# A gated linear recurrence and an ELU layer on one Trainium2 core: the decay chain of the next unit moved to other places in the order of work

## The chip, the cores and the metric

The program runs on one core of one Trainium2 chip. Its engines work side by side, each on its own queue, in order: TensorE (PE; its weight loads are listed apart as PEld), VectorE (DVE), ScalarE (ACT), GpSimd (POOL) and SyncE (SP), which here only issues DMAs. An engine that waits holds everything behind it in its queue. The metric is the device time of one execution in microseconds (us), the median of several runs.

## The reference

The first half is a linear recurrence with complex decays, for 4 batches, 8 heads, 768 steps and 48 channels a head. The second is a two-layer network with ELU between the layers, over the 3072 tokens that come out.

```python
mag = np.sqrt(a_re * a_re + a_im * a_im)
scale = np.minimum(mag, 0.999) / (mag + 1e-06)
a_re_n, a_im_n = (a_re * scale, a_im * scale)
for t in range(S):
    ar, ai = (a_re_n[:, :, t, :, None], a_im_n[:, :, t, :, None])
    new_re = ar * S_re - ai * S_im
    new_im = ar * S_im + ai * S_re
    kv = np.einsum('bhd,bhe->bhde', k[:, :, t], v[:, :, t])
    S_re, S_im = (new_re + kv, new_im)
    y[:, :, t] = np.einsum('bhd,bhde->bhe', q[:, :, t], S_re)
...
x = np.ascontiguousarray(attn_out.transpose(0, 2, 1, 3)).reshape(B * S, H * D)
h = x @ w_in            # 3072x384 by 384x2048
g = np.where(h > 0.0, h, alpha * (np.exp(np.minimum(h, 0.0)) - 1.0))
return (g @ w_out).astype(np.float32)   # 2048x384
```

## The kernel before

**Units and layers.** The work is cut into 12 units, numbered u = 0 to 11. A unit is 128 steps of two batches, all 8 heads: 256 tokens. Each unit goes through two stages. Its *front* computes the recurrence for those 128 steps. Its *layer* runs the ELU network over its 256 tokens. The front of unit u is worked during the layers of u-2 and u-1, so that TensorE always has matrix products to do.

**The front, in its steps** (function names as in the code):

- `load_a`, `load_v`, `load_qk` fetch the inputs, four or two DMAs each on SP's queue. The decays' real and imaginary parts (`ar`, `ai`) have one buffer each.
- `squares` (L709, L710): two ScalarE squares. `joined` (L716): their sum, on GpSimd for units from 3 on.
- `logarithms` (L735, L736): two ScalarE logarithms, of `ar` and of the sum. `powers` (L746, L747): two ScalarE exponentials of these.
- `lengths` (L772, VectorE): the log of the capped decay, `l`. `ratios` (L759, L760, GpSimd), `slopes` (L780, VectorE), `angles` (L815, ScalarE arctangent), `carried` (L821, VectorE) and `noted` (L796, L799, VectorE minima and maxima).
- `turns`: a TensorE sum over time of the angles (L832), rounded by VectorE (L837, L840), and the last row sent on by a GpSimd-issued DMA (`carry`, L856). `waves` (L967 to L971): sine and cosine on ScalarE.
- `scaled` (L981 GpSimd, L982 VectorE), `ends` (L951, two DMAs issued by GpSimd) and `gated` (L993, keys on GpSimd, queries on VectorE) build the gated queries and keys.
- `transposed` (L1013 TensorE, L1014 ScalarE), `scored` (L1054, L1125), then `valued`: value products (L1087), the sums of the logs of the *next* unit (`quartered`, L883, which read `l`), the carried products (L1096), the exponentials of those sums (L898, ScalarE, in `quarters_used`) and the copies of the result to SBUF (L1156, L1157, ScalarE). `seam` (L1169) then moves a part of that result across partitions with six DMAs on SP's queue. Only then is the layer's input `x` complete.

**The layer.** `hidden` is eight steps: `inner` (12 matmuls, L1189, into one of three PSUM buffers tagged `mlp`) and `elu` (L1198 and L1199 on ScalarE, L1200 on VectorE). The second product is done by a scheme with seven products k = 1 to 7 in the place of eight, each in two halves h = 0, 1 (`product`, L1295, eight matmuls a half). The order is (1,0), (4,0), (1,1), (4,1), (6,0), (6,1), (5,0), (5,1), (7,0), (7,1), (2,0), (2,1), (3,0), (3,1), as pairs (k,h). `folded` (L1273, VectorE) prepares sums of the first matrix. The products use three `mlp` banks. Products 1, 2 and 6 share the first one. After (1,1) ScalarE copies product 1 out of it into a tile `ee` (L1303):

```python
if k == 1:
    x["u"] = new("ee", 2, [C, 2, GT])
    nc.scalar.copy(out=x["u"][:, 0, 0:HN], in_=to)
    return
```

Four quarters of the result go out through two `o` buffers, by DMAs on SP's queue (L1317). The third quarter is copied to its buffer by ScalarE (L1314) after (2,1), the others come from VectorE (L1316). The first `inner` of the next layer takes over the `mlp` bank that L1314 reads.

**What sets the order.** There is no scheduler at run time. Every step is given a place, a number of slots, by `put`; the list is sorted by place (ties in the order in which they were put) and the instructions are issued in that order, each to its engine's queue. A unit has 16 slots: with r = 16 (u-2), the layer of u-2 has its eight `hidden` at r+4 to r+11 and its fourteen half products from r+12 to r+19.4, and the layer of u-1 the same 16 slots later. Up to the first products of layer 2 a list written by hand (`first`) takes the place of the numbers; it holds all of the units 0 to 3, and of unit 4 the loads, squares, sum, logarithms and powers. `PAIRED` is 4. So the chain of unit 5 is the first that the numbers place from its squares on; this chain lies in layer 3, and that of unit 11, the last, in layer 9.

Of the kernel before, what the change touches and what calls it, by code (L numbers as in the profile page):

```python
# [505 lines left out]
def kernel(  # L506
# [19 lines left out]
    NU = B // NB * (S // C)  # L526
# [472 lines left out]
    PAIRED = 4  # L999
# [404 lines left out]
    def put(at, fn, *args):  # L1404
        if fn is hidden:
            plan.append((at, len(plan), inner, args))
            plan.append((at, len(plan), elu, args))
        else:
            plan.append((at, len(plan), fn, args))

    def decays_of(u, *at):
        fns = squares, logarithms, powers, lengths, ratios, slopes, noted, angles, carried
        put(at[0], begun, u)
        for x, fn in zip(at, fns):
            put(x, fn, u)
            if fn is squares:
                put(x, joined, u)

    def gates_of(u, *at):
        for x, fn in zip(at, (decays, turns, waves, scaled, ends, gated)):  # L1420
            if fn is not decays or u <= PAIRED:
                put(x, fn, u)

    def values_of(u, *at):
        fns = (transposed, "q"), (transposed, "k"), (scores,), (states,), (values,)
        for n in range(NB):
            for x, (fn, *key) in zip(at[5 * n :], fns):
                put(x, fn, u, *key, n)
        put(at[-1], seam, u)
# [64 lines left out]
    def layer_of(u, at_h, at_p):  # L1494
        for m in range(NF // 2):
            put(at_h[m], hidden, u, 2 * m)
        put(at_h[3], folded, u, 0)
        put(at_h[7], folded, u, 1)
        ks = [(1, 0), (4, 0), (1, 1), (4, 1)] + [(k, h) for k in (6, 5, 7, 2, 3) for h in range(2)]
        for m, (k, h) in enumerate(ks):  # L1500
            put(at_p[0] + m * len(at_p) / len(ks), product, u, k, h)

    for u in range(2, NU):
        r = (u - 2) * SLOTS
        put(r + 8, load_a, u)
        put(r + 8, load_v, u)
        put(r + 8, load_qk, u)
        if u == 2:
            decays_of(u, 16, 17, 17, 18.4, 19.5, 19.6, 22.7, 19.8, 19.8)
            gates_of(u, 20.4, 21.6, 22.1, 22.4, 22.4, 22.6)  # L1510
        else:
            decays_of(u, r + 11, r + 12, r + 12, r + 13.4, r + 13.5, r + 14.9, r + 16.7, r + 15.5, r + 16.6)
            gates_of(u, r + 15, r + 18, r + 18.5, r + 18, r + 18, r + 19.5)
        if u < PAIRED:
            values_of(u, *(max(r + 22, 24.5) + x for x in (0, 1, 2, 3, 5, 4, 5, 6, 7, 8, 9)))
        else:
            for n in range(NB):
                put(r + 22 + 2 * n, transposed, u, "q", n)
                put(r + 23 + 2.3 * n, transposed, u, "k", n)
            put(r + 26.6, scored, u)  # L1520
            put(r + (31 if u + 1 < NU else 29.3), valued, u)
            put(r + (31 if u + 1 < NU else 29.3), seam, u)
        layer_of(u, range(r + 36, r + 44), range(r + 44, r + 52))
    for m in range(NR):
        put(40 + 4 * m, test_fetch, m)
# [42 lines left out]
```

## Time and profile before

| what | value |
|---|---|
| median of 3 runs | 730.74 us (727.02 to 731.93) |
| the profiled execution: its own time | 733.4 us |
| its span, first to last instruction | 731.7 us |
| mean granted TensorE clock | 0.966 |
| TensorE busy | 677.1 us, 93% |
| weight loads busy | 593.2 us, 81% |
| ScalarE, VectorE, GpSimd busy | 398.5, 395.9, 176.0 us |

The profile is of one execution. Busy shares are averages over stages with different limits, and what an engine loses is read from the waits: for each group of instructions, how long its engine sat idle before it, and which instruction of which engine ended that. In rows of the order in time, the columns are start, length, engine, line, operation, tiles written and read, shapes, and how many were merged into the row; a bracket at the end is the idle time before it. PEclk is the clock that was granted to TensorE as a share of full speed.

### The profile page before, as it was taken

What the parts mean: (1) busy time and instruction counts of PE and PEld (TensorE: products, weight loads), DVE (VectorE), ACT (ScalarE), POOL (GpSimd) and SP (SyncE); (2) the same over time, 40 slices, a digit from 0 to 9 for tenths busy, and PEclk for the clock granted to TensorE, in tenths of its full rate; (3) what the DMA queues carried; (4) which work ended last, traced back from release to release, by engine and by line L of the source; (5) the groups of instructions that cost most, each with busy time, mean ns of one, the idle gap of its engine ahead of it and who ended that gap; (6) DMA issues with size and microseconds to landing.
All of it is one profiled execution on the core that took longest, in us unless ns stands there. A gap on an engine that the chain in (4) does not pass through costs nothing.

```text
span 731.7 us, 15769 instructions
## 1 busy us (share of the span) xinstructions
PE 677.1 (93%) x6656; PEld 593.2 (81%) x6656; DVE 395.9 (54%) x579; ACT 398.5 (54%) x622; POOL 176.0 (24%) x159
## 2 busy tenths in 40 slices
PE   8798899988999979979979998997997997999996
PEld 6787775665889879879879887997987986989995
DVE  5789999516666545454454553553644545433141
ACT  6765446578466456645653754655546654661230
POOL 2000000237145133151331431422413403310000
PEclk9889999999999989989999999998999999999999
DMA  9986555232536403701901901920730550200000
GB/s 166 168 144 110 141 172 130 51 61 50 77 77 110 93 23 88 115 22 49 154 23 40 142 23 33 152 41 25 125 77 22 116 86 24 72 1 7 22 1 27
DMA packets 149899, 55.98 MB, mean 77 GB/s; under 512 B 129172, under 2 KB 142652, under 8 KB 149820
## 3 DMA queue, kind: packets, MB, share of 16 engines
q1 hardware_dynamic: 147776, 54.32, 39.1%
q0 software_dynamic: 1824, 0.44, 0.8%
q8 instruction: 54, 0.88, 0.5%
q14 instruction: 25, 0.20, 0.1%
q10 hardware_dynamic: 220, 0.14, 0.1%
HBM read 48.88 MB, written 4.78 MB: 73 GB/s over the span
## 4 chain that ended last, share of the span: by engine, by line
PE 73%; issue 6%; ACT 5%; DVE 5%; POOL 5%; SPq 3%; DMA 2%; ACTq 0%; POOLq 0%; DVEq 0%
PE mlp L1189 28%; PE mlp L1295 22%; PE w L1013 5%; PE mlp L1210 4%; PE y L1096 3%; PE w L1054 2%; POOL n L716 2%; SPq L596 2%; PE y L1125 2%; PE y L1087 2%; PE w L832 2%; POOL S L1071 1%; PE w L1210 1%; ACT n L746 1%; ACT n L736 1%
## 5 line engine op out<-in xcount | busy, mean ns | idle before, releaser
L1189 PE MATMUL mlp<-x,w_in 128*128 128x256 f32 x1152 | 260.6, 381 | 2.6 <-DVE g L1200 2.6
L1189 PEld LDWEIGHTS mlp<-x,w_in 128*128 128x128 f32 x1152 | 214.6, 190 | 31.9 <-DVE g L1200 3.0
L1198 ACT ACTIVATE ee<-mlp 128x512 f32<-128x512 f32 x96 | 57.3, 597 | 144.1 <-PE mlp L1189 135.8
L1200 DVE SCALAR_TENSOR_TENSOR g<-ee,mlp 128x512 f32<-128x512 f32 x96 | 65.5, 685 | 126.2 <-ACT ee L1199 116.6
L1295 PE MATMUL mlp<-w_out,g 128*128 128x192 f32 x640 | 110.3, 326 | 0.0
L1295 PEld LDWEIGHTS mlp<-w_out,g 128*128 128x128 f32 x640 | 105.4, 190 | 2.7
L1295 PE MATMUL mlp<-w,g 128*128 128x192 f32 x320 | 70.5, 384 | 28.4 <-ACT ee L1303 28.4
L1295 PEld LDWEIGHTS mlp<-w,g 128*128 128x128 f32 x320 | 64.3, 227 | 31.9 <-ACT ee L1303 30.5
L1071 POOL TENSOR_TENSOR S<-S,T 128x384 f32<-128x384 f32 x36 | 29.3, 830 | 168.4 <-DVE S L1069 168.4
L1273 DVE TENSOR_TENSOR g<-g 128x512 f32<-128x512 f32 x80 | 67.2, 841 | 2.7
L1199 ACT ACTIVATE ee<-ee 128x512 f32<-128x512 f32 x96 | 60.5, 631 | 2.9
L898 ACT ACTIVATE n<-w 64x384 f32<-64x384 f32 (+1 forms) x60 | 28.1, 486 | 49.3 <-PE w L883 48.6
L856 POOL DMA_DIRECT2D carry<-n x10 | 5.3, 530 | 172.9 <-DVE n L840 172.9
L993 POOL TENSOR_TENSOR kg<-k,cs 128x1536 f32<-128x1536 f32 x9 | 41.0, 4551 | 20.1 <-issue 20.0
L1314 ACT COPY o<-mlp 128x192 f32<-128x192 f32 x10 | 3.2, 319 | 67.1 <-DMA out_dram<-o 56.3
L821 DVE SCALAR_TENSOR_TENSOR n<-carry,n 1x768 f32<-1x768 f32 x10 | 9.5, 946 | 45.3 <-ACT n L815 45.3
L1210 PE MATMUL mlp<-w_out,g 128*128 128x384 f32 x96 | 32.8, 490 | 0.7 <-DVE g L1200 0.7
L1014 ACT COPY qt<-w 128x512 f32<-128x512 f32 x48 | 25.6, 581 | 12.5 <-PE w L1013 12.5
L1295 PE MATMUL mlp<-wt,g 128*128 128x192 f32 x160 | 29.2, 327 | 0.0
L993 DVE TENSOR_TENSOR qg<-q,cs 128x1536 f32<-128x1536 f32 (+1 forms) x12 | 19.5, 1623 | 17.4 <-ACT cs L971 17.4
L716 POOL TENSOR_TENSOR n<-n 128x768 f32<-128x768 f32 x9 | 19.8, 2196 | 35.4 <-ACT n L710 35.4
L1013 PE MATMUL w<-ident,kg 128*128 128x128 f32 x192 | 26.0, 280 | 2.3 <-POOL kg L993 1.4
(173 smaller groups left out, 981.4 us busy)
## 6 DMA issues: line engine op xcount, KB each, us to landing
w<-in_moe_w_out_dram SPq DMA_DIRECT2D x8, 768.0 KB, 4.9
g<-in_moe_w_in_dram SPq DMA_DIRECT2D x16, 384.0 KB, 3.2
g<-in_moe_w_out_dram SPq DMA_DIRECT2D x16, 384.0 KB, 3.4
w<-in_moe_w_in_dram SPq DMA_DIRECT2D x16, 288.0 KB, 5.9
vn<-in_v_dram SPq DMA_DIRECT2D x24, 192.0 KB, 4.0
out_dram<-o SPq DMA_DIRECT2D x48, 96.0 KB, 2.1
ar<-in_a_re_dram SPq DMA_DIRECT2D x22, 192.0 KB, 4.6
ai<-in_a_im_dram SPq DMA_DIRECT2D x22, 192.0 KB, 7.5
```

The source lines that it names most:

```text
L716: products(u).tensor_tensor(out=x["m2"], in0=x["m2"], in1=x["sq"], op=ALU.add)
L898: nc.scalar.activation(out=flat(x[key][to, n : n + 1]), in_=t[of], func=AF.Exp, scale=sign)
L993: eng.tensor_tensor(out=to[:, :, :, 0:D], in0=each.unsqueeze(2).to_broadcast([C, step * H, 2, D]), in1=x["cs"][:, n * H : (n + step) * H], ...
L1013: nc.tensor.transpose(t[:, h], of, ident)
L1071: eng.tensor_tensor(out=new_s, in0=new_s, in1=wide, op=ALU.mult)
L1189: nc.tensor.matmul(t[:, e], lhsT=w_in[:, i, ts(f + e, C)], rhs=x["x"][:, i], start=(i == 0), stop=(i == NI - 1),)
L1198: nc.scalar.activation(out=e, in_=t, func=AF.Relu, scale=-1.0)
L1199: nc.scalar.activation(out=e, in_=e, func=AF.Exp, scale=-1.0)
L1200: nc.vector.scalar_tensor_tensor(out=x["g", f // 8][:, f % 8 : f % 8 + 2], in0=e, scalar=-1.0, in1=t, op0=ALU.add, op1=ALU.max)
L1210: nc.tensor.matmul(x["o", n], lhsT=x["g", f // 8][:, f % 8, ts(n, C)], rhs=w_out[:, f], start=(f == 0), stop=(f == NF - 1),)
L1273: nc.vector.tensor_tensor(out=S_of(u, k, h), in0=a, in1=b, op=op)
L1295: nc.tensor.matmul(to, lhsT=a[:, m], rhs=b[:, m], start=(first and h == 0 and m == 0), stop=False, skip_group_check=True,)
```

## The change

Five steps get other places. For units from 5 on:

- `load_a` is issued at the start of layer u-2 (r+4) and not in its middle (r+8).
- `squares` moves from the end of layer u-2's `hidden` (r+11, ahead of the first product) to r+7.2, behind its fourth `hidden`. `joined`, which shared the place of the squares, gets its own, r+8.4, behind the fifth.
- `powers` moves from r+12, right behind `logarithms`, to r+13.2: behind half product (1,1), and so behind that product's ScalarE copy (L1303), and ahead of (4,1).

For units from 4 on `valued` and `seam` move from r+31 to r+31.6, that is, from ahead of half product (5,0) to behind it, and with that from ahead of the next unit's `angles` to behind them (not for the last unit). `turns` moves from r+18 to r+18.6: behind half product (2,1), and behind `scaled` and `ends`, which it was ahead of. `waves` moves from r+18.5 to r+19, behind (3,0).

```diff
     def decays_of(u, *at):
-        fns = squares, logarithms, powers, lengths, ratios, slopes, noted, angles, carried
+        fns = squares, joined, logarithms, powers, lengths, ratios, slopes, noted, angles, carried
         put(at[0], begun, u)
         for x, fn in zip(at, fns):
             put(x, fn, u)
-            if fn is squares:
-                put(x, joined, u)
...
-        put(r + 8, load_a, u)
+        put(r + (4 if u > PAIRED else 8), load_a, u)
         put(r + 8, load_v, u)
         put(r + 8, load_qk, u)
         if u == 2:
-            decays_of(u, 16, 17, 17, 18.4, 19.5, 19.6, 22.7, 19.8, 19.8)
+            decays_of(u, 16, 16, 17, 17, 18.4, 19.5, 19.6, 22.7, 19.8, 19.8)
             gates_of(u, 20.4, 21.6, 22.1, 22.4, 22.4, 22.6)
         else:
-            decays_of(u, r + 11, r + 12, r + 12, r + 13.4, r + 13.5, r + 14.9, r + 16.7, r + 15.5, r + 16.6)
-            gates_of(u, r + 15, r + 18, r + 18.5, r + 18, r + 18, r + 19.5)
+            decays_of(u, r + 7.2, r + 8.4, r + 12, r + 13.2, r + 13.4, r + 13.5, r + 14.9, r + 16.7, r + 15.5, r + 16.6)
+            gates_of(u, r + 15, r + 18.6, r + 19, r + 18, r + 18, r + 19.5)
...
-            put(r + (31 if u + 1 < NU else 29.3), valued, u)
-            put(r + (31 if u + 1 < NU else 29.3), seam, u)
+            put(r + (31.6 if u + 1 < NU else 29.3), valued, u)
+            put(r + (31.6 if u + 1 < NU else 29.3), seam, u)
```

## The prediction

> **What bounds the kernel now.** I read first the page's busy shares (TensorE 93% of the span, the others under 55%), then what TensorE waits for, longest in total first (us in total, times, longest):
>
> ```profile
> PE mlp L1295 <- ACT ee L1303: 28.4, 7, 4.1
> PE mlp L1189 <- DVE g L1200: 2.6, 1, 2.6
> PE w L883 <- DVE n L772: 2.4, 2, 1.3
> ```
>
> One wait holds nearly everything that TensorE loses in the second half: seven times about 4.06 us, once in each of layers 3 to 9, before half product (6,0), for ScalarE's copy of product 1. The order in time around the one in layer 5, TensorE and then ScalarE, shows why the copy is late:
>
> ```profile
> 376.94 1.46 PE L1295 MATMUL mlp<-w_out,g 128*128 128x192 f32 x8
> 378.24 1.46 PE L1295 MATMUL mlp<-wt,g 128*128 128x192 f32 x8
> 383.76 4.55 PE L1295 MATMUL mlp<-w,g 128*128 128x192 f32 x16 [4.06 <-ACT ee L1303]
> ...
> 375.71 0.83 ACT L709 ACTIVATE n<-ar 128x768 f32<-128x768 f32 x1
> 376.44 0.83 ACT L710 ACTIVATE n<-ai 128x768 f32<-128x768 f32 x1
> 377.29 1.28 ACT L735 ACT_TABLE_LOAD   x1
> 378.58 0.84 ACT L735 ACTIVATE n<-ar 128x768 f32<-128x768 f32 x1
> 379.68 0.84 ACT L736 ACTIVATE n<-n 128x768 f32<-128x768 f32 x1 [0.26 <-POOL n L716]
> 380.54 1.28 ACT L746 ACT_TABLE_LOAD   x1
> 381.84 0.94 ACT L746 ACTIVATE n<-n,ln_eps 128x768 f32<-128x768 f32 x1
> 382.68 0.83 ACT L747 ACTIVATE n<-n 128x768 f32<-128x768 f32 x1
> 383.41 0.30 ACT L1303 COPY ee<-mlp 128x192 f32<-128x192 f32 x1
> ```
>
> Product (1,1) is done at 378.2, but squares, logarithms and powers stand ahead of its copy, which ends at 383.7. The stall costs more than itself. The same stretch in windows of 1 us gives the granted clock in the last columns but two:
>
> ```profile
> 384.00:385.00 1.00, 1.00 (x7) 1.00 (x7) 0.00 (x0) 0.00 (x0) 1.00 (x1) 0.87 0.12 36
> 385.00:386.00 1.00, 1.00 (x5) 1.00 (x4) 0.00 (x0) 0.00 (x0) 0.92 (x2) 0.50 0.00 0
> ```
>
> The clock is halved for 3.4 us, in other layers for 6.8. Eight matmuls take 1.30 us at full clock (376.94 to 378.24), so 16 take 2.6; after the seven stalls they take 5.49, 5.25, 4.55, 4.35, 5.26, 4.54 and 4.31 in the chain that ended last, 33.75 together, and the value products behind them another 0.7 over their 1.09 each. That is 33.75 - 18.2 + 0.7 = 16.2 us. So 28.4 + 16.2 = 44.6 us hang on this copy.
>
> **The change part by part, in layer 5's times.**
>
> *Squares and sum earlier.* ScalarE stands idle about 1.25 us ahead of each `elu` in the layer; the two squares (1.56 us together) use one such gap and push one `elu` by some 0.3 us, against three PSUM buffers. GpSimd has nothing between 353.4 and 370.25, so the 2.30 us of the sum fit. It will slow `folded` there (VectorE's four took 2.87 us alone, 4.37 beside the sum), which VectorE's idle of 2.3 to 2.8 us ahead of each L1200 takes up. Cost nothing; were the cover gone, about 1 us a layer.
>
> *The loads earlier.* SP issues the four loads of `ar` and `ai` at 405.19 to 409.13, right behind the last output, although their place is the middle of the layer: SP runs ahead. So the move only passes them by one test fetch (0.39 us), which then goes 3.9 us later, for a test some ten us away. The values are read about 14 us after the layer's start, and they land about 7.5 us after issue. Nothing gained or lost; the price, if they were late, is ScalarE held in the squares, behind which TensorE has some 5 us of free buffers.
>
> *Powers behind the copy.* ScalarE's last `elu` ends at 375.80. Then come a table load (1.28), two logarithms (0.84 each, 0.09 overlapped), and the copy: 378.63 to 378.93. Half product (4,1) ends at 379.70. The copy is 0.75 us early, so the wait and the clock's drop both go: 6.37 us a layer (44.6/7).
>
> *What is late next.* Powers, and all that hangs on them, are now on ScalarE's queue ahead of the exponentials of `valued`, because `angles` comes before `valued`. The chain from the copy's end, each by its row:
>
> 1. table 378.95 to 380.23, powers (0.94, 0.83) to 381.91.
> 2. `ratios` on GpSimd, 1.86 + 1.80 with a gap: to 385.73. `slopes` on VectorE 0.95: 386.72.
> 3. `angles` 0.84: 387.59. Its table load hides in ScalarE's wait. Layer 1 shows that order, and shows the load that must follow, since the exponentials come after an arctangent:
>
> ```profile
> 164.88 1.28 ACT L815 ACT_TABLE_LOAD   x1
> 167.19 0.84 ACT L815 ACTIVATE n<-n 128x768 f32<-128x768 f32 x1 [1.03 <-DVE n L780]
> ...
> 168.48 1.28 ACT L898 ACT_TABLE_LOAD   x1
> ```
>
> 4. That load (one more a layer than before) to 388.88, six exponentials 2.9: 391.8; the copies of `valued` 1.13: 392.93.
> 5. `seam`, then a test fetch, on SP. The outputs of products (7,1) are ready at about 392.3 in the new order, but stand behind them:
>
> ```profile
> 394.16 3.68 SPq L1169 DMA_DIRECT2D x<-y  x6
> 397.93 0.53 SPq L665 DMA_DIRECT2D g<-in_moe_w_in_dram  x1
> 399.67 4.95 SPq L1317 DMA_DIRECT2D out_dram<-o  x4
> ...
> 401.83 0.32 ACT L1314 COPY o<-mlp 128x192 f32<-128x192 f32 x1 [5.55 <-DMA out_dram<-o]
> ```
>
>    `seam` 392.96 to 396.64, fetch to 397.26, first output issued 397.35. L1314 needs that output's buffer, 2.16 us after issue: 399.51, done 399.83. The next layer's first `inner` needs the bank that L1314 reads (by the code; before, L1314 was 1.7 us early and the trace shows no wait): 399.9.
>
> TensorE itself, with no wait, reaches that `inner` sooner: (6,0) and (6,1) end at 382.3 in place of 388.31, and the rest up to the layer's start is unchanged work, 403.86 - 388.31 = 15.5: 397.8. So a new stall of about 2.1 us opens at the head of the next layer, 2.2 with the small gaps between engines. Its bounds: should the bank not bind, `x` itself does (last `seam` DMA 396.64 + 1.8 landing), 0.6; were each of the eight hand-overs 0.1 slower, 3.0. I take 2.2, since each term has its own row.
>
> *Values, turns, waves later.* `quartered` needs `lengths`: powers' first exponential ends at 381.18, L772 0.96 later, and TensorE comes there at 384.6: free. Without the move it would wait, as before layer 2 (1.1 us at L883). `turns` behind `scaled` and `ends` takes GpSimd's carry DMA (0.54) behind 1.84 + 1.93; the carry is wanted two units on, and the gated keys are better off. It puts the sums' four matmuls (1.29) one half product later, no longer in all. `waves` starts after L1314 at 399.85 and ends at 403.7, 3.8 us into the next layer (before: 2.1); the first `elu` frees its bank about 7.1 us in, TensorE wants it 8.6 us in. Free, with 1.5 us to spare.
>
> *Two rules against the rows.* The Trainium skill, "ScalarE: Activation LUTs", section "What ACT_TABLE_LOAD costs", counts 1283 ns for a load and 1380 more for a drain[...]; that speaks against powers apart from the exponentials of `valued`. Here a load takes 1.28 us and the next activation starts 0.01 us after it (377.29 + 1.28, 378.58). By the rule the copy would come 0.65 us late for TensorE and the chain behind it would grow by two drains, 2.8: a head stall of 5.0, with a clock drop of 2.3, 7.95 against 6.37 a layer, 11 us slower in all. I take the row.
>
> "TensorE: Matmul & The Clock Gate", section "What's actually happening", has the clock drop after an idle window of 3.4 us, windows running on their own. By that a stall of 2.2 never costs clock. I laid windows of 3.41 us on the trace's record of the clock: each window of layers 3 to 9 with 2.12 us or more without matmuls was followed by half clock, and two with 1.92 and 1.94 us kept the half clock that they had; those with up to 1.89 us were not. The wait of 2.63 us at 76 us was split 1.54 and 1.09 and cost nothing. So the bound lies near 1.9. A stall of 2.2 puts that much into one window in (3.41 - 2.2 + 2 × 0.3) / 3.41 = 53% of its positions: 4 of 7 layers, 1.7 us each (half of 3.4), 6.8 us. By the rule the result is 7 us better; I take the trace.
>
> **The sum.** Gain 44.6; new stalls 7 × 2.2 = 15.4; clock 6.8. Net 22.4 us. The profiled execution goes from 733.4 (span 731.7 and 1.7 around it) to 711.0. The runs' median is 2.7 lower: 730.7 - 22.4 = 708.3, so 708.
>
> **The rivals.**
>
> - *Head stall replaces a part* (the forecast), 0.80. Stall 1.4 and no clock drop gives 730.7 - 44.6 + 9.8 = 696; 3.0 and a drop each time 730.7 - 44.6 + 21 + 12 = 719.
> - *All of it gained*, 0.06: the outputs or L1314 don't bind, or the chain is shorter by a link: 730.7 - 44.6 = 686, 690 with the stall of 0.6. For: layer 2 has the copy ahead of the logarithms and no stall. Against: there `seam` isn't on SP's queue.
> - *It doesn't do what it says*, 0.06: the copy is held by something else (the logarithm waiting for GpSimd's sum, say), or the head stall equals the old one: within 1%, 731. Against: in the new order the sum has ten us to spare.
> - *Slower*, 0.08: the chain powers, `ratios`, `angles`, exponentials, `seam`, output grows. GpSimd beside VectorE can take half as long again as alone (2.30 for the sum in layer 5 against 1.84 in layer 2), so `ratios` may cost 1.8 more, and the arctangent's table load 1.28 if it doesn't hide. The stall is then 5.3 with two cold windows (3.4): 8.7 - 6.4 = 2.3 × 7, 747. It decides at a stall of 4.1.
>
> A change of under 1% either way, 723.4 to 738.0, is about what a measurement here can't tell from none. Faster: 0.80 + 0.06 = 0.86; same 0.06; slower 0.08. The range is that of the first case, a little wider at its ends for the runs' own spread (727.0 to 731.9): 692 to 720.
>
> **What would show it.** Right: no wait L1295 on L1303; a wait of L1189 at each layer's first `inner` from layer 4 to 10, about 2.2 us, ended by L1314; L898 with a table load of its own; half clock in some layer heads and none at (6,0). Wrong: that wait at 4 us or at 0; a wait at L883 on L772, or at the fourth `inner` on L1200 (waves too late); squares waiting for `ai`.

## The result, and the profile after

The changed kernel takes 703.17 us (median of 4 runs, 702.64 to 703.51) beside 731.05 us before: a ratio of 0.963, with a 95% interval of 0.959 to 0.967. That is 27.9 us faster. The forecast was 708, with a range of 692 to 720. The profiled execution took 702.64 us with a span of 700.9, against 733.4 and 731.7, and the mean granted clock rose from 0.966 to 0.990.

What TensorE waits for after the change, longest first (us in total, times, longest), and two rows of the same view for its weight loads:

```profile
PE mlp L1189 <- DMA x<-y: 5.1, 8, 1.1
PE mlp L1189 <- DVE g L1200: 4.2, 8, 2.4
PE w L883 <- DVE n L772: 2.4, 2, 1.3
PE w L1013 <- DVE qg L993: 2.1, 8, 0.7
...
PEld mlp L1189 <- DVE g L1200: 6.3, 8, 2.8
...
PEld mlp L1189 <- ACT o L1314: 2.6, 7, 0.6
```

The seven waits of 4.06 us on the copy L1303 are gone. In their place are small ones at the heads of layers 4 to 10 (a head is a layer's first `inner` steps), none over 1.1 us: for `x`, for L1314, for the gated queries, for the first `elu`. The 2.4 us in the second line is an early wait that the kernel before has too (2.6). L883 on L772 is as it was, in the layers that the change doesn't touch.

The order in time around layer 5's products, TensorE and then ScalarE:

```profile
363.84 1.46 PE L1295 MATMUL mlp<-w_out,g 128*128 128x192 f32 x8
...
366.44 1.46 PE L1295 MATMUL mlp<-w_out,g 128*128 128x192 f32 x8
367.74 1.46 PE L1295 MATMUL mlp<-wt,g 128*128 128x192 f32 x8
369.04 4.06 PE L1295 MATMUL mlp<-w,g 128*128 128x192 f32 x24
...
368.10 0.30 ACT L1303 COPY ee<-mlp 128x192 f32<-128x192 f32 x1
368.41 1.28 ACT L746 ACT_TABLE_LOAD   x1
...
376.23 0.84 ACT L815 ACTIVATE n<-n 128x768 f32<-128x768 f32 x1 [3.55 <-DVE n L780]
377.09 1.28 ACT L898 ACT_TABLE_LOAD   x1
```

The copy stands right behind the logarithms. It ends 0.64 us before the row behind half product (4,1) starts, and the 24 matmuls of that row follow with no gap at full clock, 4.06 us. But ScalarE now stands 3.55 us idle for `slopes` in front of the arctangent, with the exponentials of `valued` behind it. The head of the next layer, SyncE's queue, ScalarE, then TensorE:

```profile
382.45 3.68 SPq L1169 DMA_DIRECT2D x<-y  x6
386.23 0.53 SPq L665 DMA_DIRECT2D g<-in_moe_w_in_dram  x1
386.86 4.70 SPq L1317 DMA_DIRECT2D out_dram<-o  x4
...
390.40 0.32 ACT L1314 COPY o<-mlp 128x192 f32<-128x192 f32 x1 [7.98 <-DMA out_dram<-o]
...
387.75 8.47 PE L1189 MATMUL mlp<-x,w_in 128*128 128x256 f32 x36 [0.39 <-DMA x<-y]
396.42 1.09 PE L1013 MATMUL w<-ident,qg 128*128 128x128 f32 x8 [0.20 <-DVE qg L993]
397.78 2.86 PE L1189 MATMUL mlp<-x,w_in 128*128 128x256 f32 x12 [0.26 <-DVE g L1200]
```

The first `inner` starts at 387.75, long before L1314 ends at 390.72. Before the change the 36 matmuls took 7.93 us; here they take 8.47, with a gap inside.

### The profile page after: what moved, and what is told of

It is laid out like the page before. It is cut to its first block, busy times and chain, and to the rows that moved or that the text cites. A ratio compares the mean times of both kernels' runs of the same rounds, so it can differ in the third digit from the quotient of the medians.

```text
span 700.9 us, 15768 instructions
## 1 busy us (share of the span) xinstructions
PE 667.1 (95%) x6656; PEld 577.9 (82%) x6656; DVE 407.3 (58%) x579; ACT 403.3 (58%) x629; POOL 178.8 (26%) x159
## 4 chain that ended last, share of the span: by engine, by line
PE 67%; DVE 10%; ACT 9%; issue 5%; DMA 4%; POOL 2%; SPq 1%; DVEq 0%; POOLq 0%; ACTq 0%
PE mlp L1189 22%; PE mlp L1295 21%; PE w L1013 5%; PE mlp L1210 4%; DMA out_dram<-o 3%; PE y L1096 3%; PE w L1054 2%; PE y L1125 2%; DVE qg L993 2%; ACT L967 2%; PE y L1087 2%; DVE g L1200 1%; DVE n L840 1%; DVE rnd L837 1%; PE w L1210 1%
## 5 line engine op out<-in xcount | busy, mean ns | idle before, releaser
L1189 PE MATMUL mlp<-x,w_in 128*128 128x256 f32 x1152 | 265.0, 384 | 9.6 <-DMA x<-y 5.1
L993 POOL TENSOR_TENSOR kg<-k,cs 128x1536 f32<-128x1536 f32 x9 | 45.0, 4995 | 60.6 <-issue 60.6
L1295 PE MATMUL mlp<-w,g 128*128 128x192 f32 x320 | 56.0, 329 | 0.0
L1295 PEld LDWEIGHTS mlp<-w,g 128*128 128x128 f32 x320 | 52.0, 190 | 1.5 <-issue 0.6
L1314 ACT COPY o<-mlp 128x192 f32<-128x192 f32 x10 | 3.2, 318 | 85.2 <-DMA out_dram<-o 74.4
L759 POOL TENSOR_TENSOR n<-ar,n 128x768 f32<-128x768 f32 x9 | 16.6, 1845 | 61.3 <-ACT n L747 61.3
L680 DVE TENSOR_REDUCE seen<-g 128x1 f32<-128x384 f32 x32 | 17.5, 546 | 24.3 <-DMA g<-in_moe_w_out_dram 14.4
L716 POOL TENSOR_TENSOR n<-n 128x768 f32<-128x768 f32 x9 | 18.1, 2008 | 48.7 <-ACT n L710 48.7
```

The source lines that it names most:

```text
L993: eng.tensor_tensor(out=to[:, :, :, 0:D], in0=each.unsqueeze(2).to_broadcast([C, step * H, 2, D]), in1=x["cs"][:, n * H : (n + step) * H], ...
L1189: nc.tensor.matmul(t[:, e], lhsT=w_in[:, i, ts(f + e, C)], rhs=x["x"][:, i], start=(i == 0), stop=(i == NI - 1),)
L1295: nc.tensor.matmul(to, lhsT=a[:, m], rhs=b[:, m], start=(first and h == 0 and m == 0), stop=False, skip_group_check=True,)
```

## The experiments

All times are medians; each ratio is to runs of the kernel before on the same chip, with its 95% interval. Those runs took 731.92 us beside powers alone, loads, squares and sum alone, the long filler, and values back ahead of the angles; 731.04 us beside the other four. The theory: the copy's wait and the halved clock behind it are the whole gain, and the loss at the heads comes from `angles` standing ahead of `valued`'s exponentials.

**Powers alone.** The kernel before, with one number changed.

```diff
-            decays_of(u, r + 11, r + 12, r + 12, r + 13.4, ...)
+            decays_of(u, r + 11, r + 12, r + 13.2, r + 13.4, ...)
```

> The kernel before with powers alone moved to r+13.2. Theory (the copy's wait is the whole gain, and the loss at the layers' heads comes from valued standing behind angles): ScalarE's squares (to 377.3), table load and logarithms, the last of them held by GpSimd's sum, stay ahead of the copy, which ends near 380.8 in layer 5's times; TensorE waits 1.1 us for it in place of 4.06, too short for a clock drop; valued stays ahead of angles, its exponentials need no table load, and no loss opens at the heads. 731 - 44.6 + 7 x 1.1 = 694. Rival (powers behind the copy make all behind them late, wherever valued stands): the head loss of about 1.9 us a layer is there too, 707, with waits at L883 on L772.

Measured 698.31 us, ratio 0.955 (0.953 to 0.957): one of the five moves is faster than all of them together. Its waits of TensorE begin so:

```profile
PE mlp L1295 <- ACT ee L1303: 7.6, 7, 1.1
PE w L883 <- DVE n L772: 2.4, 2, 1.3
```

The wait is 1.1 us, as expected; there is no new wait at L883 (the two shown are those of the kernel before), none at the heads of layers 4 to 10, and no clock drop. The theory's 694 is missed by 4. About half of that shows in the trace: from one layer's first product to the next it takes 53.14 us, where the kernels with no such wait (those with `angles` behind `valued`, below) take 51.80. So a wait of 1.08 us costs 1.34, and seven of them 9.4 us and not 7.7. The rest is within the spread of its runs (696.8 to 700.1). The rival's head loss isn't there.

**Loads, squares and sum alone.** The kernel before, with the first two parts of the change and nothing else. `load_a` and `joined` have their lines of the change too, not shown here.

```diff
-            decays_of(u, r + 11, r + 12, r + 12, r + 13.4, ...)
+            decays_of(u, r + 7.2, r + 8.4, r + 12, r + 12, r + 13.4, ...)
```

> The kernel before with load_a, squares and joined inside the layer, all else in its old place. Theory: the copy still stands behind two table loads, two logarithms and two exponentials and ends near 381.95, a wait of about 2.3 us in place of 4.06 in layers 3 to 9; in about half of them a clock drop of 1.7 us; no loss at the heads: 731 - 44.6 + 16 + 6 = 708, between 703 (no drop) and 714 (a drop each time). Rival (the squares were the larger part of the gain): at or below the 703 of the whole change.

Measured 707.42 us, ratio 0.967 (0.965 to 0.968). The wait is 2.2 us, and its rows show what a wait of that length does to the clock, in two layers:

```profile
261.76 4.39 PE L1295 MATMUL mlp<-w,g 128*128 128x192 f32 x16 [2.22 <-ACT ee L1303]
...
373.59 2.87 PE L1295 MATMUL mlp<-w,g 128*128 128x192 f32 x16 [2.22 <-ACT ee L1303]
```

The same wait, and once the 16 matmuls behind it take 1.5 us longer. The granted clock (last columns but two) in 3.4 us behind each:

```profile
262.90:266.30 3.40, 3.40 (x19) 2.96 (x21) 0.04 (x1) 0.00 (x0) 2.34 (x2) 0.50 0.00 0
...
374.40:377.80 3.40, 3.40 (x85) 2.91 (x83) 0.97 (x2) 0.00 (x0) 2.68 (x2) 1.00 0.02 5
```

The clock was halved behind three of the seven. Windows of 3.41 us laid on the trace's record of the clock, as in the prediction, held 2.22, 2.03 and 2.10 us without matmuls ahead of those three, and 1.76 us or less in the other four layers.

**The clock alone.** The kernel before, with matmuls of the identity, read by nobody, to fill the wait.

```diff
+    def kept_busy(u):
+        t = work([C, C])
+        for _ in range(26):
+            nc.tensor.matmul(t, lhsT=ident, rhs=ident, start=True, stop=True)
...
+        if 3 <= u <= 9:
+            put(at_p[0] + 3.4 * len(at_p) / len(ks), kept_busy, u)
```

> The kernel before with 26 matmuls of the identity put between half products (4,1) and (6,0) of layers 3 to 9, which fill about 2.8 of the 4.06 us wait and add no work that anything reads. Theory: the wait is as long, the clock isn't halved behind it, and 16.2 us go: 715. Rival (the slow matmuls behind the wait are slow for another reason): 731, with 16 matmuls of L1295 still taking 4.3 to 5.5 us.

Measured 730.30 us, ratio 0.998 (0.996 to 1.000). The filler was mis-sized. Each call became two instructions of 0.11 us, so it took 5.8 us where the wait was 4.06:

```profile
377.13 5.97 PE L1405 MATMUL w<-ident 128*128 128x128 f32 x52
382.93 2.77 PE L1295 MATMUL mlp<-w,g 128*128 128x192 f32 x16
```

The 16 matmuls behind it did run at full clock, 2.77 us. What that gave, the overlong filler took: about 1.75 us by seven, 12 us. A filler of half the size fits the wait:

> The kernel before with 13 matmuls of the identity, half of the earlier filler, between half products (4,1) and (6,0) of layers 3 to 9: 26 matmul instructions of 0.11 us, 2.8 of the 4.06 us wait. Theory (the slow matmuls behind the wait are the halved clock): the rest of the wait, about 1.2 us, stays on L1303, the 16 matmuls of (6,0) and (6,1) take 2.6 to 2.8 us, and 16 us go: 716. Rival: 731.

Measured 718.61 us, ratio 0.982 (0.979 to 0.985).

```profile
374.92 3.06 PE L1405 MATMUL w<-ident 128*128 128x128 f32 x26
379.14 2.87 PE L1295 MATMUL mlp<-w,g 128*128 128x192 f32 x16 [1.15 <-ACT ee L1303]
```

The copy is as late as ever: TensorE goes on 4.06 us behind (4,1) (375.08 to 379.14), and only the clock has changed: 12.4 us in the runs, 12.8 between the two spans (731.7 and 718.9). That no work was saved, and matmuls were added, makes this the plainest of the runs. It is 3 to 4 us short of the 16.2 that the sum had; the last part says why.

**Values back ahead of the angles.** The changed kernel with `valued` and `seam` at r+31.

```diff
-            put(r + (31.6 if u + 1 < NU else 29.3), valued, u)
-            put(r + (31.6 if u + 1 < NU else 29.3), seam, u)
+            put(r + (31 if u + 1 < NU else 29.3), valued, u)
+            put(r + (31 if u + 1 < NU else 29.3), seam, u)
```

> The changed kernel with valued and seam back at r+31, ahead of half product (5,0) and of angles. Theory (the loss of 1.9 us at each head comes from angles ahead of valued's exponentials: the wait for ratios and slopes, one more table load, then seam and the outputs on SP's queue): lengths are ready at about 382.1, TensorE comes to L883 at 383.3, so no wait there; seam is issued some 4 us earlier, the first output and L1314 2 us earlier, waits of L1189 on x and on L1314 go: 703 - 7 x 1.9 = 690. Rival (valued has to stand later because its sums need lengths, which powers now hold up): a wait of 1 us or more at L883 on L772 in each layer, and 703 to 711.

Measured 688.75 us, ratio 0.942 (0.940 to 0.943): 14 us below the whole change.

```profile
PE w L883 <- DVE n L772: 2.4, 2, 1.3
...
383.08 7.93 PE L1189 MATMUL mlp<-x,w_in 128*128 128x256 f32 x36
```

There is no new wait at L883, so `valued` had no need to go later, and layer 6's first `inner` waits for nothing.

**Angles behind the values.** The changed kernel with one number changed; TensorE's order stays that of the change.

```diff
-            ... r + 14.9, r + 16.7, r + 15.5, r + 16.6)
+            ... r + 14.9, r + 16.7, r + 15.7, r + 16.6)
```

> The changed kernel with the next unit's angles at r+15.7, behind valued, which stays at r+31.6 behind half product (5,0). TensorE's order is that of the changed kernel; only ScalarE's order of the arctangent and the six exponentials is turned round. Theory (angles ahead of the exponentials cost the layers' heads): the exponentials start when TensorE's sums end, about 5 us sooner than in the changed kernel, with no table load of their own, and the waits of L1189 on x and L1314 go: 689, as with valued at its old place. Rival (the place of valued behind (5,0) costs by itself): 700 to 703.

Measured 687.21 us, ratio 0.940 (0.937 to 0.943). This is the sharper of the two, since only ScalarE's order of two steps is turned round. In its rows the exponentials wait for TensorE's sums and nothing else, and SyncE issues `seam` 15.1 us after the first product starts (357.52), not 18.6 (363.84 to 382.45):

```profile
368.58 2.37 ACT L898 ACTIVATE n<-w 128x384 f32<-128x384 f32 x5 [3.52 <-PE w L883]
...
372.62 1.28 ACT L815 ACT_TABLE_LOAD   x1
...
372.63 3.69 SPq L1169 DMA_DIRECT2D x<-y  x6
...
380.87 7.93 PE L1189 MATMUL mlp<-x,w_in 128*128 128x256 f32 x36
```

The first `inner` waits for nothing. Two things went together here, the exponentials' wait behind the arctangent and their own table load (1.28 us at 377.09 in the changed kernel); no run parts them. This kernel, and the two with `valued` at r+31, are faster than both the kernel before and the change; which of the three is fastest, their intervals don't tell.

**The test fetch behind the outputs.** The changed kernel, where SyncE's queue has the test fetch no longer between `seam` and the outputs.

```diff
-        put(40 + 4 * m, test_fetch, m)
-        put(43 + 4 * m, test)
+        late = {2: (3.8, 3.2), 3: (2.6, 2), 0: (1.2, 0)}.get(m % 4, (0, 0)) if m > 5 else (0, 0)
+        put(40 + 4 * m + late[0], test_fetch, m)
+        put(43 + 4 * m + late[1], test)
```

> The changed kernel with the test fetch that stands between seam and the outputs on SP's queue put behind the outputs, and its test, the next fetch and the next test later in step. Theory (the heads wait for the first output's landing, which holds L1314, the waves and the gated queries): the first output is issued 0.5 us sooner and lands in some 2.2 us, not 3.5, with no fetch under way; L1314 1.9 us sooner; what is left at a head is the wait for x, 0.5: 694. Rival (seam's landing, x, is what binds): at most 0.5 us a layer gained, 700 to 703.

Measured 694.31 us, ratio 0.949 (0.945 to 0.952). Its queue, ScalarE and TensorE at the same head:

```profile
385.26 3.53 SPq L1317 DMA_DIRECT2D out_dram<-o  x4
...
387.64 0.32 ACT L1314 COPY o<-mlp 128x192 f32<-128x192 f32 x1 [6.20 <-DMA out_dram<-o]
...
386.93 8.01 PE L1189 MATMUL mlp<-x,w_in 128*128 128x256 f32 x36 [0.54 <-DMA x<-y]
394.77 1.04 PE L1013 MATMUL w<-ident,qg 128*128 128x128 f32 x8
```

The output lands and frees L1314 2.4 us after its issue (2.0 to 2.5 over the seven layers), against 3.5 (3.3 to 3.6) with a fetch right ahead of it. The waits for L1314, for the queries and for the first `elu` go, and the wait for `x` stays (4.6 us in total). So about half of the head loss (8.9 of 16.0 us between the runs' medians) came through the first output and L1314, and the rest through `seam` itself.

**Turns and waves back too.** The kernel with `valued` and `seam` at r+31, and with the old places of these two.

```diff
-            gates_of(u, r + 15, r + 18.6, r + 19, r + 18, r + 18, r + 19.5)
+            gates_of(u, r + 15, r + 18, r + 18.5, r + 18, r + 18, r + 19.5)
```

> The changed kernel with valued and seam at r+31 and also turns and waves at their old places r+18 and r+18.5. Theory (their move is covered on every engine): 689 within 2 us of the kernel with valued and seam alone put back. Rival (the move was needed, because the carry DMA ahead of scaled and ends holds GpSimd's keys): 692 or more, with waits of L1013 on GpSimd's gated keys.

Measured 688.57 us, ratio 0.942 (0.939 to 0.945), beside 0.942 with them moved. Their move does nothing that a measurement here can tell. TensorE's waits for the keys on GpSimd are the same single one as before:

```profile
PE w L1013 <- POOL kg L993: 1.4, 1, 1.4
```

## Why the prediction was right, and where it was off

**The copy's wait: right.** Measured as the prediction did, against the end of half product (4,1) (369.20), the copy came 0.80 us early, where 0.75 was worked out. With the heads' loss taken away (angles behind the values) the kernel is 43.8 us faster than before, against the 44.6 of the sum. The traces say the same without the parts that the change leaves alone. These are the first products of layers 3 and 10, before, after the change, and with angles behind the values:

```profile
256.46 1.46 PE L1295 MATMUL mlp<-w_out,g 128*128 128x192 f32 x8
663.91 1.46 PE L1295 MATMUL mlp<-w_out,g 128*128 128x192 f32 x8
...
255.76 1.46 PE L1295 MATMUL mlp<-w_out,g 128*128 128x192 f32 x8
633.79 1.46 PE L1295 MATMUL mlp<-w_out,g 128*128 128x192 f32 x8
...
253.51 1.46 PE L1295 MATMUL mlp<-w_out,g 128*128 128x192 f32 x8
616.50 1.46 PE L1295 MATMUL mlp<-w_out,g 128*128 128x192 f32 x8
```

That is 407.5, 378.0 and 363.0 us: 44.5 gained, and 15.0 of it lost again at seven heads. Squares and loads alone leave a wait of 2.2 us, powers alone one of 1.1, so each of the two moves is needed for the whole, and the move of powers is worth more.

**The clock behind it: right in kind, and about 2 us too large.** The short filler gained 12.4 us with the copy as late as before. That is less than 16.2, and most of the difference is a slip in the sum. It set the length of rows of 16 matmuls against twice 1.30, which is the time from the start of one row of eight to the start of the next. A row of 16 at full clock has a length of 2.87 (379.14 with the short filler). So 7 × 0.27 = 1.9 us of the 16.2 belong to the wait itself, which costs that much more than its length, as powers alone shows too, and 14.3 us are left for the clock. The 44.6 of the two together stays as it is. Between the first products of layers 3 and 10 the short filler gains 13.1 us. Of the 1.2 that are left, 1.05 stand in one layer (57.17 us, where the others behind the first take 56.12).

**What is late next: right, in its place and nearly its size.** The chain was predicted link by link. From the start of the first product, `seam` should be issued after 18.62 us and was after 18.61; the first output after 23.01 and was after 23.02. The loss that it opens was put at 7 × 2.2 = 15.4 us; the runs give 703.17 - 687.21 = 16.0, the traces 15.0. The rule on a drain behind each table load, which the prediction set against its rows and by which the change would have been slower, was rightly left: the load at 368.41 takes 1.28 us, the activation behind it starts at 369.71, and the chain kept its times. In the case for "slower", GpSimd's "half as long again" is more than its own figures give (2.30 against 1.84 is a quarter); `ratios` took 1.85 and 1.82 us in the changed kernel.

**Where it failed: two steps.** The first is "the next layer's first `inner` needs the bank that L1314 reads". It doesn't, and so the description of the kernel before is wrong there too: the first `inner` runs from 387.75, while L1314 reads until 390.72. It was held by `x` alone, 0.4 us in this layer, which is the lower bound that the prediction gave (0.6). It is the second `inner` that waits for L1314, as its weight loads show:

```profile
388.24 2.02 PEld L1189 LDWEIGHTS mlp<-x,w_in 128*128 128x128 f32 x10 [0.22 <-issue]
390.77 0.51 PEld L1189 LDWEIGHTS mlp<-x,w_in 128*128 128x128 f32 x3 [0.51 <-ACT o L1314]
```

The first `inner` got another bank, which must be product 4's, read last at about 381.9: the banks seem to be handed on in the order in which they come free, not in turn. That reading was not tried by itself. The second is the output's landing, put at 2.16 us and measured at 3.5 (386.86 to 390.40). The 2.16 came from a row where the fetch had been issued 1.74 us ahead of the output (397.93 and 399.67); in the new order it is 0.63 (386.23 and 386.86). With it L1314, the waves, the gated queries and the first `elu` are all later, so TensorE also waits at the queries and at the fourth `inner`, where the prediction had 1.5 us to spare and named such a wait as a sign that it was wrong. That the two errors cancelled in the sum is luck: one stall of 2.2 us became four pieces with work between them, in layer 6 0.39 us for `x`, 0.51 in the weight loads for L1314, 0.20 for the queries and 0.26 for the first `elu`, and a mean of 2.15 us a layer in all.

That is why the clock term was wrong, and the total with it. "4 of 7 layers, 1.7 us each, 6.8 us" held for one stall of 2.2 us, and it does hold where there is one: squares and loads alone show three of seven. After the change no window of 3.41 us in the heads held more than 1.0 us without matmuls, and the clock stayed full. 27.9 us in place of 22.4 is this term: 6.8 us more from it, 0.8 less from the copy (43.8 for 44.6) and 0.6 less from the heads (16.0 for 15.4).

**Covered parts: right.** Squares inside the layer, the earlier loads, turns and waves cost nothing that the runs show. The reason that the prediction gave for the move of `valued` was half right: TensorE comes to the sums after `lengths` at either place, so the move wasn't needed. Behind `angles` it cost 14.4 us (703.17 - 688.75), of some 43 that the rest gained.

## What to carry to other kernels

When a step is put behind another on an in-order engine, follow what is now behind *it*: here two exponentials moved past one copy, and one arctangent, which waits for three other engines, then stood ahead of the work that feeds the next layer. A step that waits long belongs behind the steps that are ready, even if only by one place. And price a stall with its clock: with loads, squares and sum alone, a wait of 2.22 us made a layer 2.5 us longer where the clock stayed (54.29 us against 51.80 with no wait) and 4.1 us where it fell (55.88). After the change the 2.15 us a layer, in pieces, never cost clock.

## What the runs showed of the hardware that was not expected

- A wait of 2.2 us was enough to halve TensorE's clock for 3.4 us in three layers of seven. In layers 3 to 9 of the kernel before and of loads, squares and sum alone, each window of 3.41 us that held 2.03 us or more without matmuls (59%) was followed by half clock, and no window at full clock with 1.89 us or less. A window already at half clock follows no such bound here: the prediction names two, with 1.92 and 1.94 us, that kept it, but in layer 3 before (265.3 to 268.7) one with 0.6 us kept it too, behind a window with no matmul at all. The prediction passes over that one, and its cause is open.
- Filling most of a wait with matmuls that nobody reads made the kernel 12 us faster.
- An output's landing took 3.5 us with a fetch issued 0.63 us ahead of it on the same queue, 2.4 with the fetch behind it, and 2.16 with a fetch 1.74 us ahead (before). What delays it was not tried.
- VectorE's product of the queries (L982) took 2.14 us in each of the seven layers of the changed kernel, where it starts beside GpSimd's of the keys (L981), and 0.95 us before, where it doesn't. No wait of TensorE names it.
